# Stores of half batches 0 to 8 moved from ScalarE to SyncE, and one more step in the background work at the start of the expert layers

## The chip, the core and the metric

The kernel runs on one core of one Trainium2 chip. A core has engines that run side by side and wait for each other by semaphores: TensorE (PE, matmuls), VectorE (DVE), ScalarE (ACT), GpSimd (POOL) and SyncE (SP, which only issues transfers here). SyncE, ScalarE and GpSimd issue DMA transfers, each into a queue of its own; 16 DMA engines carry them out. The metric is the device time of one execution in microseconds (us), lower is better.

## The reference

A causal convolution of width 7 over 8 batches of 3584 tokens with 192 channels, with weights that are a softmax per head, is followed by a mixture of 8 experts. Each token is given to one expert by going through all gate logits in falling order until an expert is full (28672 / 8 = 3584 tokens).

```python
w = exp(weight - weight.max(-1)); w = w / (w.sum(-1) + 1e-9)          # 8 heads x 7
x_unf = x_pad[:, arange(S)[:, None] + arange(7)]                      # sliding windows
a = einsum('hk,bskhg->bshg', w, x_unf).reshape(N, D)                  # N = 28672, D = 192

logits = a @ w_gate                                                   # N x 8
for idx in argsort(-logits.flatten()):                                # greedy, with capacity N // 8
    tok, e = idx // E, idx % E
    if assigned[tok] < 0 and counts[e] < cap:
        assigned[tok] = e; counts[e] += 1
for e in range(E):
    m = assigned == e
    out[m] = maximum(a[m] @ w1[e], 0) @ w2[e]                         # 192 x 1024, 1024 x 192
```

All of it is float32; the kernel splits operands into high and low parts where the matmul's precision needs it.

## The kernel before

**The convolution.** The tokens are cut into 16 half batches of 1792. `load(i)` brings the half batch into one of four `X` buffers, by transfers that SyncE issues (lines 189 or 192, and 194) and, for the second half of the windows, one that ScalarE issues (line 194, put off through `later`). `conv(i)` multiplies by a Toeplitz matrix `TH`, one matmul group `cv` for each of 8 heads, ScalarE copies each result into `a` (one of three buffers), and after the last head the whole `a` is stored to `attn` in DRAM, line 214. The experts' inputs are gathered from `attn` later. Half batch 14's store is held back and issued in half batch 15. Loads run three half batches ahead: in program order stands `load(i + 3)`, then `conv(i)` with its store.

**The gate.** Beside the convolution of the next half batches, VectorE transposes `a` (`transp`, tile `aT`), TensorE makes gate logits from it (`gate(i, u)`, u = 0 to 2, tile `pl`, or `bg` when a bank of the background work is used), ScalarE brings them to tile `L`, and `end(i)` transposes `L` with one matmul (`pt<-ident,L` or `bg<-ident,L`), stores it in `LT` and reduces it (`M`).

**The routing** is background work: a list of generators, `bg = Steps(..., (half(0), tail(), half(1), rest()))`. Each `yield` in them ends a step; the main program calls for a step at places that it chooses. `half(0)` works on the tokens of the first 8 half batches while the later ones are convolved, and ends with the indices of the first tiles; its matmuls use banks named `bg` (`bg<-iq,ones` and `bg<-c_oh,X` among the last). `tail()` finishes the gate of half batches 14 and 15.

**The experts.** 56 tiles of 512 tokens, 7 for each expert: first layer `ph`, 8 groups of five matmuls; `hh` and `hl`, its high and low parts; second layer `y`. `wload` (lines 1235 to 1240) brings weights to tile `raw` by SyncE, and ScalarE and VectorE make `w` and `dl` of them. The first four pieces of these loads are called when half batch 13 begins, behind the last loads of `X` in SyncE's order. In tile 0 the main program asks for background steps three times in each of the first layer's eight groups, and only the calls whose numbers are in `TAIL = (6, 7, 8, 11, 12)` (line 1497) take one.

**What sets the order.** Each engine carries out its instructions in the order of the program. DMAs from SyncE and ScalarE take eight semaphores, DMAHW0 to DMAHW7, in turn, in the order in which the program lists them; a DMA waits until the transfer that used its semaphore before has landed. In the rows of the order below `[waits ...]` names the semaphores that an instruction waits for.

Of the kernel before, what the change touches and what calls it, by code (L numbers as in the profile page):

```python
# [18 lines left out]
PEW, PEA = "pe", "pe after act"  # L19
# [95 lines left out]
def build(ctx, tc, nc, x, weight, wg, attn, LT, wk):  # L115
# [4 lines left out]
    V, A, PE, P = nc.vector, nc.scalar, nc.tensor, nc.gpsimd  # L120
# [81 lines left out]
    def conv(i, mid, hold=None):  # L202
        t = X.pop(i)
        a = AA[i] = k.ap[i % 3].tile([128, 16, D], F32, name="a")
        o = a.rearrange("p w (h c) -> p h w c", c=24)
        for h in range(8):
            ps = k.cps.tile([128, 512], F32, name="cv")
            PE.matmul(ps[:, 0:384], TH[0:118, h], t[:, :, h * 24:(h + 1) * 24], start=True, stop=True)
            mid(h)
            A.activation(o[:, h], ps[:, 0:384].rearrange("p (w c) -> p w c", c=24), AF.Copy)  # L210
        put = partial(A.dma_start, attn[i * 1792:(i + 1) * 1792].rearrange("(g p b) d -> p g (b d)", g=4, b=4),
                      a[0:W].rearrange("p (g b) d -> p g (b d)", b=4))
        if hold is None:
            put()  # L214
        else:
            hold.append(put)
# [24 lines left out]
    def logits_t(i):  # L241
# [5 lines left out]
        A.activation(o, v, AF.Copy)  # L247

    k.load, k.conv, k.transp, k.logits, k.logits_t = load, conv, transp, logits, logits_t
    k.toeplitz, k.gate_load, k.gate_ops = toeplitz, gate_load, gate_ops  # L250
    return k
# [1248 lines left out]
def moe_kernel(ctx, tc, x, weight, wg, w1, w2, out):  # L1500
    nc = Pace(tc.nc)
# [4 lines left out]
    attn = drm.tile([NTOK, D], F32, name="attn")  # L1506
    with ExitStack() as cw:
# [52 lines left out]
        def tail():  # L1560

            end(14)
            for u in range(3):
                gate(15, u)
                yield PEA if u == 2 else None
            end(15)
            nc.sync.dma_start(r.ltab, LT)
            c1.close()
            cs.close()
            ff.wpool2(cw, 1)  # L1570
            ff.hp[1] = pool(cw, "fh1", 1, **late)
            yield

        bg = Steps(nc, r, (half(0), tail(), half(1), rest()))
        bg.keep = 3
        cs, c1, ca, cl, cc = (ExitStack() for _ in range(5))
# [20 lines left out]
        def end(i):  # L1597

            k.logits_t(i)
            r.top(i)  # L1600
# [9 lines left out]
        def gate(i, u):  # L1610
            for f in range(2 * u, 2 * u + 2):
                k.logits(i, f)
# [156 lines left out]
```

## Time and profile before

| | us |
|---|---|
| median of 3 runs | 1238.71 |
| lowest and highest run | 1238.25, 1239.27 |
| the profiled execution's own time | 1242.89 |
| its span in the profile | 1241.1 |

The profile is of one execution; times in it count from the start of the span. Engine names with a q (ACTq, SPq) are an engine's issuing of transfers. In a row of the timeline stand start and length in us, engine, line of the kernel, operation, output and inputs by the program's names, shapes, the number of instructions, and in brackets the idle time of the engine ahead of it with what ended it. Most compute instructions go through one helper and so have line 56. In the profile the conv stage lasts until about 155 us, and the tiles of the experts fill the rest.

The costliest groups of instructions (columns: line, engine, operation, tiles, count | busy us, mean ns | idle us of the engine just before them, with what ended most of it) are the experts' matmuls; the convolution's come far behind:

```profile
L56 PE MATMUL y<-w,hh 128*128 128x384 f32 x1792 | 535.7, 355 | 0.0
...
L56 PE MATMUL ph<-xa,w 128*128 128x512 f32 x1344 | 395.2, 402 | 0.4 <-DVE hl L56 0.4
...
L56 PE MATMUL cv<-X,TH 118*128 118x384 f32 x256 | 99.7, 516 | 13.9 <-DVE TH L56 12.2
```

### The profile page before, as it was taken

Reading aid. Unit: us, or ns where it says so; the run is one execution under the profiler, and the core shown is the slowest. Engines: PE = TensorE matmul, PEld = TensorE weight load, DVE = VectorE, ACT = ScalarE, POOL = GpSimd, SP = SyncE. Lnnn points to the kernel's source line nnn. Section 1 sums busy time; section 2 is a strip of 40 time slices with the busy share of each in tenths; the row PEclk is TensorE's granted clock in tenths of the full one; section 3 lists DMA queues with packets and bytes.
Section 4 is the critical chain, followed back from the end, with each engine's and each line's share of the span. In section 5 each row is a group of like instructions: output and inputs, shape, how many; then the busy total and the mean of one; then the engine's idle time right before and its main releaser. Section 6 shows DMA issues by size and latency. Waiting matters only on the chain.

```text
span 1241.1 us, 21785 instructions
## 1 busy us (share of the span) xinstructions
PE 1203.0 (97%) x7694; PEld 1033.9 (83%) x7694; DVE 984.8 (79%) x2126; ACT 559.6 (45%) x1251; POOL 532.5 (43%) x520
## 2 busy tenths in 40 slices
PE   6999899999999999999999999999999999999997
PEld 3545578889989988889888889999999999999996
DVE  7588679898998988889879856777777777777762
ACT  5544555556445454444554443343333433333332
POOL 2000234435556555555465435434544444543422
PEclk9999999999999999999999999999999999999999
DMA  9999664659427473745343442114223232423100
GB/s 249 369 347 325 202 215 121 151 159 323 140 68 215 134 244 83 255 155 184 102 130 105 126 106 70 45 39 158 94 100 105 100 101 93 155 69 125 48 24 28
DMA packets 128580, 182.00 MB, mean 147 GB/s; under 512 B 20992, under 2 KB 91088, under 8 KB 126800
## 3 DMA queue, kind: packets, MB, share of 16 engines
q1 hardware_dynamic: 85856, 104.13, 27.6%
q0 software_dynamic: 21504, 44.07, 12.0%
q10 hardware_dynamic: 21104, 32.34, 7.6%
q8 instruction: 62, 1.02, 0.3%
q14 instruction: 54, 0.44, 0.1%
HBM read 102.37 MB, written 78.12 MB: 145 GB/s over the span
## 4 chain that ended last, share of the span: by engine, by line
PE 87%; DVE 5%; DMA 4%; issue 1%; ACT 1%; ACTq 0%; SPq 0%; POOL 0%; POOLq 0%; DVEq 0%
PE ph L56 40%; PE y L56 39%; PE cv L56 4%; PE bg L56 3%; DMA attn<-a 3%; DVE X L56 1%; PE pl L56 1%; DVE TH L56 1%; DVE aT L56 1%; DVE hl L56 1%; DMA X<-otab 0%; PE px L56 0%; DMA wb<-in_weight_dram 0%; ACTq L214 0%; DMA otab<-X 0%
## 5 line engine op out<-in xcount | busy, mean ns | idle before, releaser
L56 PE MATMUL y<-w,hh 128*128 128x384 f32 x1792 | 535.7, 355 | 0.0
L56 ACT ACTIVATE hh<-ph 128x512 fp32r<-128x512 f32 x448 | 267.3, 597 | 453.1 <-PE ph L56 380.3
L56 PE MATMUL y<-w,hl 128*128 128x192 f32 x1792 | 448.9, 251 | 0.0
L56 DVE SCALAR_TENSOR_TENSOR hl<-ph,hh 128x512 fp32r<-128x512 f32 x448 | 307.6, 687 | 129.1 <-ACT hh L56 99.7
L56 PE MATMUL ph<-xa,w 128*128 128x512 f32 x1344 | 395.2, 402 | 0.4 <-DVE hl L56 0.4
L56 PEld LDWEIGHTS y<-w,hl 128*128 128x128 f32 x1792 | 340.9, 190 | 16.2
L56 PEld LDWEIGHTS y<-w,hh 128*128 128x128 f32 x1792 | 336.3, 188 | 20.9 <-issue 3.0
L1383 POOL DMA_INDIRECT out_dram<-yo,ia x128 | 144.3, 1127 | 240.2 <-DVE yo L56 195.7
L56 PEld LDWEIGHTS ph<-xa,w 128*128 128x128 f32 x1344 | 218.5, 189 | 21.6 <-issue 1.8
L1383 POOL DMA_INDIRECT out_dram<-yo,ib x96 | 94.9, 988 | 221.0 <-DVE yo L56 213.6
L56 PE MATMUL ph<-xd,w 128*128 128x512 f32 x448 | 177.3, 396 | 0.0
L1308 POOL DMA_INDIRECT xg<-attn,ja x128 | 141.5, 1106 | 78.9 <-issue 39.1
L56 PE MATMUL ph<-xd,dl 128*128 128x512 f32 x448 | 174.1, 389 | 0.2 <-issue 0.2
L56 DVE STREAM_TRANSPOSE xs<-xg 32x128 f32<-32x128 f32 (+2 forms) x408 | 164.8, 404 | 6.6
L56 ACT ACTIVATE yt<-y 128x192 f32<-128x192 f32 x224 | 73.0, 326 | 109.8 <-PE y L56 72.3
L56 DVE TENSOR_TENSOR yo<-y,yt 128x192 f32<-128x192 f32 x224 | 79.2, 354 | 49.9 <-ACT yt L56 46.6
L1308 POOL DMA_INDIRECT xg<-attn,jb x96 | 103.3, 1076 | 29.3 <-issue 29.3
L56 PE MATMUL cv<-X,TH 118*128 118x384 f32 x256 | 99.7, 516 | 13.9 <-DVE TH L56 12.2
L56 PEld LDWEIGHTS ph<-xd,dl 128*128 128x128 f32 x448 | 84.2, 188 | 20.1 <-issue 0.5
L56 PEld LDWEIGHTS ph<-xd,w 128*128 128x128 f32 x448 | 84.0, 187 | 19.6 <-issue 0.6
L56 PEld LDWEIGHTS cv<-X,TH 118*128 118x128 f32 x256 | 44.9, 195 | 43.7 <-POOL TH L152 12.0
L56 ACT ACTIVATE a<-cv 128x384 f32<-128x384 f32 x128 | 59.4, 493 | 43.1 <-PE cv L56 21.3
(237 smaller groups left out, 919.8 us busy)
## 6 DMA issues: line engine op xcount, KB each, us to landing
attn<-a ACTq DMA_DIRECT2D x16, 1344.0 KB
raw<-in_moe_w_dram SPq DMA_DIRECT2D x56, 192.0 KB
X<-in_x_dram SPq DMA_DIRECT2D x15, 672.0 KB
X<-in_x_dram ACTq DMA_DIRECT2D x15, 672.0 KB
kw<-w SPq DMA_DIRECT2D x36, 256.0 KB
kv<-w SPq DMA_DIRECT2D x24, 384.0 KB
scr<-xs SPq DMA_DIRECT2D x96, 96.0 KB
w<-kw SPq DMA_DIRECT2D x6, 1536.0 KB
```

What stands on the lines that cost most here:

```text
L56: return f(*a, **k)
L1308: self.nc.gpsimd.indirect_dma_start(out=t[:, b], out_offset=None, in_=self.attn[0:rows], in_offset=bass.IndirectOffsetOnAxis(ap=idx[b], ax ...
L1383: st = self.nc.gpsimd.indirect_dma_start(out=self.out, out_offset=bass.IndirectOffsetOnAxis(ap=idx, axis=0), in_=o, in_offset=None, bounds ...
```

## The change

The store of a half batch is issued by SyncE for half batches 0 to 8, and by ScalarE, as before, for 9 to 15. In `tail()` a `yield` is added behind `end(14)`, so that the first logits of half batch 15, `gate(15, 0)`, are a step of their own.

```diff
@@ -208,7 +208,7 @@
             PE.matmul(ps[:, 0:384], TH[0:118, h], t[:, :, h * 24:(h + 1) * 24], start=True, stop=True)
             mid(h)
             A.activation(o[:, h], ps[:, 0:384].rearrange("p (w c) -> p w c", c=24), AF.Copy)
-        put = partial(A.dma_start, attn[i * 1792:(i + 1) * 1792].rearrange("(g p b) d -> p g (b d)", g=4, b=4),
+        put = partial((nc.sync if i < 9 else A).dma_start, attn[i * 1792:(i + 1) * 1792].rearrange("(g p b) d -> p g (b d)", g=4, b=4),
                       a[0:W].rearrange("p (g b) d -> p g (b d)", b=4))
         if hold is None:
             put()
@@ -1560,6 +1560,7 @@
         def tail():
 
             end(14)
+            yield PEW
             for u in range(3):
                 gate(15, u)
                 yield PEA if u == 2 else None
```

The order of SyncE's instructions, at the end of the convolution's loads. Rows are: line, operation, output and input, shape. Before, the last loads of `X` and the first loads of the experts' weights:

```order
L192 DMA X<-in_x_dram 6x16x192 [waits DMAHW4_49,DMAHW1_49,PE_49]
L194 DMA X<-in_x_dram 112x8x192 [waits DMAHW3_49]
L1235 DMA raw<-in_moe_w_dram 128x512 [waits DMAHW4_49]
L1237 DMA raw<-in_moe_w_dram 64x512 [waits DMAHW5_49]
L1238 DMA raw<-in_moe_w_dram 64x512 [waits DMAHW6_49]
L1235 DMA raw<-in_moe_w_dram 128x512 [waits DMAHW0_49]
L1237 DMA raw<-in_moe_w_dram 64x512 [waits DMAHW1_49]
L1238 DMA raw<-in_moe_w_dram 64x512 [waits DMAHW2_49]
```

The same place in the changed kernel:

```order
L192 DMA X<-in_x_dram 6x16x192 [waits DMAHW6_49,DMAHW4_49,PE_49]
L194 DMA X<-in_x_dram 112x8x192 [waits DMAHW5_49]
L1235 DMA raw<-in_moe_w_dram 128x512 [waits DMAHW6_49]
L1237 DMA raw<-in_moe_w_dram 64x512 [waits DMAHW7_49]
L1238 DMA raw<-in_moe_w_dram 64x512 [waits DMAHW0_49]
L1235 DMA raw<-in_moe_w_dram 128x512 [waits DMAHW1_49]
L1237 DMA raw<-in_moe_w_dram 64x512 [waits DMAHW2_49]
L1238 DMA raw<-in_moe_w_dram 64x512 [waits DMAHW3_49]
```

The instructions are the same, the semaphores have shifted. Before, DMAHW6 of the first L1238 was last used by the store of half batch 10 and DMAHW2 of the second by that of half batch 11. Now DMAHW6 of the first L1235 was last used by the store of half batch 11, DMAHW1 of the second L1235 by ScalarE's last load of `X`, and DMAHW3 of the second L1238 by the store of half batch 12.

SyncE again, in the middle of the changed kernel's convolution, from the fifth store on:

```order
L214 DMA attn<-a 112x4x768 [waits DMAHW7_49,Activation_49]
L189 DMA X<-in_x_dram 6x15x192 [waits DMAHW0_49,DMAHW1_49,PE_49,Pool_49]
L194 DMA X<-in_x_dram 112x8x192 [waits DMAHW2_49]
L214 DMA attn<-a 112x4x768 [waits DMAHW3_49,Activation_49]
L192 DMA X<-in_x_dram 6x16x192 [waits DMAHW4_49,PE_49]
L194 DMA X<-in_x_dram 112x8x192 [waits DMAHW6_49]
L214 DMA attn<-a 112x4x768 [waits DMAHW7_49,Activation_49]
```

Before, this stretch had the same rows without those of L214, which stood on ScalarE.

TensorE in tile 0, from the first layer's third group on (`bg<-ident,L` is the transposition in `end`, `bg<-aT,c_mu` the logits of `gate(15, u)`). Before:

```order
L56 MATMUL px<-ident,xg 128x128 x4
L56 MATMUL bg<-ident,L 128x128
L56 MATMUL bg<-aT,c_mu 32x128 x8
L56 MATMUL ph<-xa,w_1426 128x512 x3
L56 MATMUL bg<-aT,c_mu 32x128 x8
L56 MATMUL ph<-xd,w_1426 128x512
L56 MATMUL ph<-xd,dl 128x512
L56 MATMUL bg<-aT,c_mu 32x128 x8
L56 MATMUL ph<-xa,w_1426 128x512 x3
L56 MATMUL ph<-xd,w_1426 128x512
L56 MATMUL ph<-xd,dl 128x512
L56 MATMUL bg<-ident,L 128x128
```

The same place in the changed kernel:

```order
L56 MATMUL px<-ident,xg 128x128 x4
L56 MATMUL bg<-ident,L 128x128
L56 MATMUL ph<-xa,w_1426 128x512 x3
L56 MATMUL bg<-aT,c_mu 32x128 x8
L56 MATMUL ph<-xd,w_1426 128x512
L56 MATMUL ph<-xd,dl 128x512
L56 MATMUL bg<-aT,c_mu 32x128 x8
L56 MATMUL ph<-xa,w_1426 128x512 x3
L56 MATMUL ph<-xd,w_1426 128x512
L56 MATMUL ph<-xd,dl 128x512
L56 MATMUL bg<-aT,c_mu 32x128 x8
L56 MATMUL bg<-ident,L 128x128
```

Each group of logits has moved one place back behind first layer matmuls; the second `bg<-ident,L` stands where it stood, and now directly behind the last logits. The first step of `half(1)`, which was taken at the end of the calls in tile 0, now comes when tile 1 begins.

## The prediction

> **What bounds the kernel now.** I read the page first, for the span and the busy time of each engine, then busy time by stretches of 20 us, then the chain of waits, and last the single instructions of ScalarE, SyncE and TensorE between 75 and 170 us. The page:
>
> ```profile
> span 1241.1 us, 21785 instructions
> ...
> PE 1203.0 (97%) x7694; PEld 1033.9 (83%) x7694; DVE 984.8 (79%) x2126; ACT 559.6 (45%) x1251; POOL 532.5 (43%) x520
> ...
> PE ph L56 40%; PE y L56 39%; PE cv L56 4%; PE bg L56 3%; DMA attn<-a 3%; DVE X L56 1%; PE pl L56 1%; DVE TH L56 1%; DVE aT L56 1%; DVE hl L56 1%; DMA X<-otab 0%; PE px L56 0%; DMA wb<-in_weight_dram 0%; ACTq L214 0%; DMA otab<-X 0%
> ```
>
> TensorE is busy 1203.0 of 1241.1 us. The change takes no matmul away, so what it can win or lose is idle time of TensorE, 38.1 us in all. The chain (the work that ended last, followed back) is 79% first and second layer matmuls; but 3% of it, some 30 us, goes through the stores `attn<-a`. The stretches show where TensorE is idle while the convolutions run (columns: stretch, its length, busy PE, PEld, DVE, ACT, POOL with instruction counts, granted clock, DMA share, GB/s):
>
> ```profile
> 60.00:80.00 20.00, 18.21 (x166) 9.50 (x169) 19.17 (x55) 10.41 (x27) 0.25 (x1) 1.00 1.07 344
> 80.00:100.00 20.00, 16.96 (x150) 8.71 (x138) 15.90 (x33) 8.11 (x23) 0.29 (x1) 1.00 1.07 357
> 100.00:120.00 20.00, 19.63 (x203) 12.57 (x203) 17.03 (x33) 9.52 (x25) 1.94 (x3) 1.00 1.00 305
> 120.00:140.00 20.00, 20.00 (x207) 13.32 (x210) 16.71 (x41) 12.77 (x32) 1.04 (x1) 1.00 0.91 300
> 140.00:160.00 20.00, 15.95 (x189) 10.13 (x177) 11.41 (x16) 9.03 (x25) 9.91 (x11) 1.00 0.49 153
> ```
>
> PE lacks 1.79 + 3.04 + 0.37 = 5.2 us between 60 and 120, nothing from 120 to 140, and 4.05 from 140 to 160. In 60 to 100 the DMA engines are full (share 1.07), and DVE is nearly full in 60 to 80 (19.17 of 20). ScalarE's instructions between 82 and 126 us say why PE waits (columns: start, length, instruction, and idle time before it with what ended it; ACTq is ScalarE issuing a DMA):
>
> ```profile
> 82.98 3.88 ACTq L214 DMA_DIRECT2D attn<-a  x1
> 86.96 2.02 ACT L56 ACTIVATE a<-cv 128x384 f32<-128x384 f32 x5 [4.28 <-PE bg L56]
> ...
> 92.07 3.76 ACTq L214 DMA_DIRECT2D attn<-a  x1
> 95.93 0.49 ACT L56 ACTIVATE a<-cv 128x384 f32<-128x384 f32 x1 [4.00 <-DVE aT L56]
> 96.32 0.17 ACT L56 ACTIVATE tot<-bg 128x8 bf16<-128x8 f32 x1
> ...
> 103.04 0.32 ACTq L214 DMA_DIRECT2D attn<-a  x1
> ...
> 113.66 0.32 ACTq L214 DMA_DIRECT2D attn<-a  x1
> ...
> 125.07 0.32 ACTq L214 DMA_DIRECT2D attn<-a  x1
> ```
>
> The stores of half batches 8 and 9 hold ScalarE for 3.88 and 3.76 us, those of 10, 11 and 12 for 0.32. The named releasers of the copies behind them (PE, DVE) had long been done: ScalarE was stuck in its own issue. TensorE feels it here:
>
> ```profile
> 78.23 1.56 PE L56 MATMUL cv<-X,TH 118*128 118x384 f32 x4 [0.55 <-ACT a L56]
> 87.50 1.56 PE L56 MATMUL cv<-X,TH 118*128 118x384 f32 x4 [1.04 <-ACT a L56]
> 96.55 0.40 PE L56 MATMUL bg<-U,tot 128*128 128x128 bf16 x4 [1.59 <-ACT tot L56]
> ```
>
> **The change, part one: stores 0 to 8 on SyncE.** It removes nine store issues from ScalarE. The three waits above, 0.55 + 1.04 + 1.59 = 3.2 us, follow such an issue directly; the third comes from store 9, which stays on ScalarE. I expect that it shrinks too: the issues grow long only while earlier stores are unfinished in ScalarE's queue (the chain below has store 7 landing at 92.00, just as store 9 begins its 3.76), and after the change no store is in it. DVE at 19.17 of 20 in 60 to 80 will keep some of the first wait. I take **3.0 us** that convolution 10 starts earlier; the bounds are 0 (the transfers, full at 1.07, set the pace and another wait steps in) and 5.2 (all idle time of PE from 60 to 120). On SyncE a long issue holds only the X loads behind it, and PE waits for no X transfer between 20 and 160 us; I cost that at nothing, hidden by the loads' lead. Without the lead each store would cost its issue, up to 3.88.
>
> A row bears on whether the stall leaves ScalarE at all:
>
> ```profile
> 74.48 17.52 DMA attn<-a
> ...
> 84.11 0.31 SPq L194 DMA_DIRECT2D X<-in_x_dram  x1
> ```
>
> SyncE issued an X load at 84.11 in 0.31 us, inside ScalarE's 82.98 to 86.86. So the long issue belongs to ScalarE's own queue. The Trainium skill, Perfetto Trace Analysis, section "DMA Instruction — HWDGE (DVE, Sync)", says that the descriptor generator is shared between issuing engines and locked for exclusive use while one issues. By that rule ScalarE's own X loads would stand behind SyncE's stores, and the 3.0 would be near 0; the 0.31 inside the 3.88 speaks against it.
>
> **Part one goes on: the weight loads behind the stores.** The DMAs of SyncE and ScalarE share eight semaphores in turn, and each waits for the previous user of its own. Moving nine DMAs among the others shifts who waits for whom. Before:
>
> ```profile
> 113.70 0.56 SPq L1237 DMA_DIRECT2D raw<-in_moe_w_dram x1
> 115.80 0.47 SPq L1238 DMA_DIRECT2D raw<-in_moe_w_dram x1
> 120.26 0.35 SPq L1235 DMA_DIRECT2D raw<-in_moe_w_dram x1
> 120.66 0.47 SPq L1237 DMA_DIRECT2D raw<-in_moe_w_dram x1
> 125.09 0.47 SPq L1238 DMA_DIRECT2D raw<-in_moe_w_dram x1
> ...
> SPq L1238 <- DMA attn<-a: 5.5, 2, 4.0
> ```
>
> The two L1238 loads wait for the landings of stores 10 and 11 (last line: 5.5 us in all, 2 times, 4.0 the longest). After, the first load, L1235, waits for store 11 and the last, L1238, for store 12; on SyncE the four between are queued behind the first. The last is what counts, for ScalarE converts the weights in order and the routing's small matmuls hang behind it:
>
> ```profile
> 131.48 0.63 ACT L56 ACTIVATE w<-raw 128x512 fp32r<-128x512 f32 x1 [0.47 <-DMA raw<-in_moe_w_dram]
> ...
> 133.30 0.67 DVE L56 COPY X<-bg 128x1024 bf16<-128x1024 bf16 x1
> ...
> 134.59 0.27 PE L56 MATMUL bg<-iq,ones 128*128 128x256 bf16 x1
> ```
>
> ScalarE already waits 0.47 for this load. From its start at 131.48 to DVE's end at 133.97 are 2.5 us, and TensorE, in order, comes to these matmuls at 134.59, so 0.6 later than it need. Now the new time. Store 12 was issued at 125.07; with 3.0 won, at 122.1. Its landing: the sizes are
>
> ```profile
> attn<-a ACTq DMA_DIRECT2D x16, 1344.0 KB
> ```
>
> so at the 341 to 357 GB/s of a full stretch at least 1.376 MB / 357 = 3.9 us; at most what store 11 took, which was issued at 113.66 and let L1238 go at 125.09, 11.4 us. I take 6.7: the store and the five weight loads in front (128x512 and 64x512 numbers of four bytes, 0.92 MB) are 2.29 MB at 341. That is nearer the low end because the last X loads are then nearly through. So it lands at 128.8. The load after it: at least 0.13 MB / 357 = 0.4 us, at most the 6.4 from 125.09 to 131.48; I take 2.5, near the low end, as nothing is left in front of it. ScalarE's last conversion starts at 131.3, and TensorE's matmuls can start at 131.3 + 2.5 = 133.8: 0.8 us before 134.59. **Of the 3.0 us won, 2.2 are lost in a new wait of TensorE at about 132 us, and 0.8 remain.** The bounds are -5.2 (nothing lost) and, with both far ends, 122.1 + 11.4 + 6.4 + 2.5 = 142.4, +7.8.
>
> The Trainium skill, DMA: Bandwidth & Descriptors, section "Queues, rings and completion order", says that a DMA engine takes turns between queues by packets and serves each in order. By it stores 9 to 12, alone with the X halves in ScalarE's queue, would land sooner than store 11's 11.4, and the X loads behind stores in SyncE's later; the sum would move towards the 3.0 kept. No row of before shows such a mix.
>
> **Part two: the added `yield`.** It adds no instruction. It moves the transposition's matmuls in tile 0 by a step:
>
> ```profile
> 158.51 0.41 PE L56 MATMUL bg<-aT,c_mu 128*32 128x128 f32 x4
> 159.20 0.41 PE L56 MATMUL bg<-aT,c_mu 128*32 128x128 f32 x2 [0.27 <-DVE aT L56]
> 160.06 0.62 PE L56 MATMUL bg<-aT,c_mu 128*32 128x128 f32 x10 [0.46 <-DVE aT L56]
> 160.61 0.97 PE L56 MATMUL ph<-xa,w 128*128 128x512 f32 x3
> ...
> 162.75 0.65 PE L56 MATMUL bg<-aT,c_mu 128*32 128x128 f32 x16
> ...
> 165.69 0.33 PE L56 MATMUL bg<-ident,L 128*128 128x128 f32 x1 [0.95 <-ACT L L56]
> ```
>
> TensorE waits 0.27 + 0.46 = 0.73 us for DVE's transposes. With three `ph` matmuls (0.97) ahead, this is covered: **-0.7**. The bill may come at `bg<-ident,L`: five `ph` matmuls stood between the last logits and it, now none. It waits 0.95 today although they stand there; from the end of the last logits (162.75 + 0.65) to 165.69 are 2.3 us. Bounds for this wait: 0 and 2.3 in place of 0.95; I leave it at 0.95, its own row. So part two lies between -1.7 and +0.6. The routing's later steps slip by a third of a tile; that is beside a full TensorE with nothing that waits for them soon, and I cost it at 0.
>
> **Sum.** -0.8 - 0.7 = -1.5 us on the profiled execution, which took 1242.89 us (span 1241.1 and 1.8 around it). That execution is 4.2 above the median of 1238.71; I take the difference over to the median: **1237.2 us**.
>
> **The rivals.**
> - *The weight loads do not bind.* For it: store 12 has an emptier queue before it; if it lands in 4 to 5 us, TensorE keeps all. 3.0 to 4.5 + 0.7: 1233.5 to 1235.0. Against: ScalarE waits for this load already before. Chance 0.17.
> - *The weight loads come late: slower.* Place: the last L1238 behind store 12, then `w<-raw`, then TensorE's `bg<-iq`. It decides from the point where `w<-raw` starts after 132.7 (134.59 + 0.6 - 2.5): each us later is a us of TensorE. Store 12 in 9.2 and the load in 4.4, the middle between my values and the far ends, give 135.7, so 138.2 against 134.59: +3.6 - 0.7, 1241.6. For it: DMA share 0.91 to 1.00 from 100 to 140. Chance 0.14.
> - *The stores' move wins nothing in the convolutions*, because DMA at 1.07 sets the pace, or the generator is locked as in the rule above. Then store 12 is at 125.07, the conversion at 134.3, TensorE at 136.8: +2.2 - 0.7, 1240.2. Against: 84.11. Chance 0.12.
> - The forecast, -3.5 to +1.0 about 1237.2: 0.57.
>
> **How the numbers follow.** Faster by over 0.2% (2.5 us, about what a measurement here can tell from no change): the first rival and the fast edge of the forecast, 0.17 + 0.17 = 0.34. Slower: the second rival and a corner of the third, 0.16. The rest, 0.50, is within. The range for 8 in 10 runs from 1233.8, inside the first rival, to 1241.2, short of the far half of the second; the ends with both far prices (+7.8) I leave out as less than 3 in 100.
>
> **What would show it.** ScalarE has no L214 issue before store 9, and store 9 takes some 0.3. The waits at 87.50 and 96.55 are gone and PE's busy time in 80 to 100 rises from 16.96 to 19 or more. A new wait of 1 to 3 us appears before `bg<-iq` or in the convolution beside it, released through `w<-raw`, with L1238 issued late at about 129. In tile 0 the waits of 0.27 and 0.46 are gone. I am wrong if 120 to 140 stays full of TensorE work, or if TensorE waits for X.

## The result, and the profile after

The changed kernel takes **1248.25 us** (median of 6 runs, 1247.77 to 1249.42) against 1238.99 for the kernel before in 6 runs beside it (1238.25 to 1240.8): a ratio of **1.0074**, 95% interval 1.0061 to 1.0087. It is 0.74% slower. The forecast was 1237.2 us and its range ended at 1241.2. The profiled execution after took 1248.38 us, 0.1 above its median. That of before lay 3.9 above its median, so the two spans differ by 5.4 us and not by 9.3.

From the page of the changed kernel, the lines that answer to those of before; the last is the group of the convolution's matmuls (busy us, mean ns, idle us before them):

```profile
span 1246.5 us, 21787 instructions
...
PE 1204.9 (97%) x7694; PEld 1035.1 (83%) x7694; DVE 986.3 (79%) x2126; ACT 562.1 (45%) x1251; POOL 533.9 (43%) x520
...
L56 PE MATMUL cv<-X,TH 118*128 118x384 f32 x256 | 102.9, 528 | 25.8 <-DVE TH L56 12.7
```

The same 256 matmuls have 25.8 us of idle time before them (13.9 before), and take 102.9 us in place of 99.7. On the page's chain `DMA X<-in_x_dram` stands with 3%, where before, of the transfers, only the stores had such a share. By stretches of 20 us (columns as before):

```profile
60.00:80.00 20.00, 19.31 (x161) 9.61 (x159) 19.17 (x54) 10.10 (x27) 0.25 (x1) 1.00 1.07 355
80.00:100.00 20.00, 18.97 (x172) 9.95 (x171) 18.06 (x40) 9.46 (x27) 0.36 (x1) 1.00 1.02 328
100.00:120.00 20.00, 14.02 (x145) 8.91 (x144) 13.97 (x22) 6.24 (x17) 1.94 (x3) 1.00 1.06 307
120.00:140.00 20.00, 15.53 (x141) 10.65 (x140) 10.85 (x22) 7.69 (x18) 0.00 (x0) 0.98 0.92 271
140.00:160.00 20.00, 16.35 (x161) 9.30 (x162) 12.32 (x30) 9.53 (x24) 7.96 (x8) 0.85 0.48 146
```

From 60 to 100 TensorE gains what the prediction expected: its idle time falls from 4.83 to 0.69 + 1.03 = 1.72 us. From 100 to 140, where it lacked 0.37, it now lacks 5.98 + 4.47 = 10.45. The first expert tile begins at 167.35 us, 11.9 later than before (155.47). What follows it, up to the end, takes 1079.2 us against 1085.6. From 180 to 800 us TensorE is idle for 6.8 us in the profile of before and 3.2 in that of after, so a part of this difference is that the execution profiled before lay above its median; the loss itself lies ahead of tile 0. TensorE's waits, and the start of tile 0:

```profile
94.48 0.40 PE L56 MATMUL bg<-U,tot 128*128 128x128 bf16 x4 [0.26 <-ACT tot L56]
102.31 1.53 PE L56 MATMUL cv<-X,TH 118*128 118x384 f32 x4 [2.06 <-DMA X<-in_x_dram]
108.07 1.56 PE L56 MATMUL cv<-X,TH 118*128 118x384 f32 x4 [1.59 <-ACT a L56]
116.07 1.53 PE L56 MATMUL cv<-X,TH 118*128 118x384 f32 x4 [2.33 <-DMA X<-in_x_dram]
138.28 0.98 PE L56 MATMUL cv<-X,TH 118*128 118x384 f32 x2 [4.47 <-ACT a L56]
...
167.35 0.96 PE L56 MATMUL ph<-xa,w 128*128 128x512 f32 x3
...
171.95 0.62 PE L56 MATMUL bg<-aT,c_mu 128*32 128x128 f32 x10 [0.43 <-DVE aT L56]
...
176.91 0.33 PE L56 MATMUL bg<-ident,L 128*128 128x128 f32 x1 [1.16 <-ACT L L56]
```

Two of the long waits are for loads of `X`, and one is for a free buffer of `a`. The chain of waits through that place (start, length, what) tells how the loads came late, and two rows of SyncE and ScalarE show where the 4.47 comes from:

```profile
91.22 12.97 DMA attn<-a
...
104.20 11.73 DMA X<-in_x_dram
...
127.14 12.78 DMA attn<-a
...
139.94 2.75 DMA raw<-in_moe_w_dram
```

```profile
125.84 0.35 SPq L1235 DMA_DIRECT2D raw<-in_moe_w_dram  x1
...
136.74 0.63 ACT L56 ACTIVATE w<-raw 128x512 fp32r<-128x512 f32 x1 [6.85 <-DMA raw<-in_moe_w_dram]
```

Store 9, issued by ScalarE at 91.22, lands 12.97 us later. Only then does SyncE issue the `X` load at 104.20, although it needs nothing of that store: the two use the same semaphore. Its 0.69 MB take 11.73 us, and TensorE waits 2.33 at 116.07. The first weight load, L1235, waits in the same way for store 11 (4.0 us) and is issued at 125.84, 13 us later than before (112.80). It lands only at 136.7: ScalarE has stood still for it for 6.85 us, the copy of a convolution stands behind it in ScalarE's order, and TensorE waits 4.47 for that copy. The last weight load, on the chain above, waits for store 12; TensorE's waits behind it are 0.74 us at 143.83 and 0.38 at 145.12. But the lag is older than these waits. The transfers from 20 to 60 us in slices of 1 us, before and then after:

```profile
GB/s 257 242 256 260 290 303 409 396 398 382 402 396 406 353 343 369 328 325 358 345 376 386 392 397 389 380 359 247 351 396 376 373 390 387 396 391 386 392 355 296
DMA packets 12584, 14.23 MB, mean 356 GB/s; under 512 B 284, under 2 KB 10523, under 8 KB 12580
```

```profile
GB/s 256 236 252 257 263 213 193 291 220 339 407 412 337 329 290 156 254 314 388 399 418 386 375 340 245 309 387 390 376 359 362 302 231 242 360 366 392 389 392 382
DMA packets 11549, 12.81 MB, mean 320 GB/s; under 512 B 252, under 2 KB 9771, under 8 KB 11545
```

**By 60 us the changed kernel has moved 1.42 MB less**, about one store of 1.38 MB, while TensorE has lost only 0.5 us in this stretch (39.19 of 40 busy, 39.68 before). Both kernels begin near 250 GB/s, with loads alone; before reaches 400 in the seventh slice, after in the eleventh, and it falls back to 156 at 35. The chain and SyncE's queue say why:

```profile
30.70 11.97 DMA X<-in_x_dram
...
42.69 0.02 SPq L214
...
42.73 10.05 DMA attn<-a
```

```profile
24.62 0.31 SPq L214 DMA_DIRECT2D attn<-a  x1
...
42.73 0.31 SPq L214 DMA_DIRECT2D attn<-a  x1
...
52.85 5.24 SPq L214 DMA_DIRECT2D attn<-a  x1
```

Store 2, issued at 34.15 before, now stands in SyncE's queue behind `X` loads, the last of which is issued at 37.48 in 0.49 us, and then waits 4.7 us more for the semaphore of a load that ScalarE had issued at 30.70. It starts at 42.73, 8.6 us later; store 0 is 3.4 later (24.62 against 21.23).

The packets tell loads and stores apart, since those of 512 B to 2 KB are the loads' (768 B) and those of 2 to 8 KB the stores' (3072 B). Counted so, these megabytes were moved from 20 us to the time at the head of the column, in before, after and the kernel of experiment 10 below:

| | 40 us | 60 us | 100 us |
|---|---|---|---|
| loads: before, after, exp. 10 | 3.92, 3.80, 3.07 | 7.86, 7.31, 6.66 | 15.15, 13.92, 13.14 |
| stores: before, after, exp. 10 | 2.86, 1.98, 3.66 | 6.32, 5.45, 5.83 | 12.97, 12.42, 12.70 |

In the changed kernel the stores are late first, by 0.88 MB at 40 us. When they come through, the loads fall behind, by 0.55 MB at 60 us and 1.23 at 100. SyncE's half of the load for half batch 11 is issued at 89.64 (76.71 before) and that for 12 at 104.20 (84.11 before).

### The profile page after: what moved, and what is told of

It reads as the page before. It is cut to its first block, busy times and chain, and to the rows that moved or that the text cites. A ratio compares the mean times of both kernels' runs of the same rounds, so it can differ in the third digit from the quotient of the medians.

```text
span 1246.5 us, 21787 instructions
## 1 busy us (share of the span) xinstructions
PE 1204.9 (97%) x7694; PEld 1035.1 (83%) x7694; DVE 986.3 (79%) x2126; ACT 562.1 (45%) x1251; POOL 533.9 (43%) x520
## 3 DMA queue, kind: packets, MB, share of 16 engines
q0 software_dynamic: 21504, 44.07, 11.9%
## 4 chain that ended last, share of the span: by engine, by line
PE 88%; DMA 6%; DVE 3%; ACT 1%; issue 1%; POOL 0%; POOLq 0%; SPq 0%; ACTq 0%; DVEq 0%
PE ph L56 41%; PE y L56 39%; PE cv L56 3%; DMA X<-in_x_dram 3%; DMA attn<-a 3%; PE bg L56 3%; DVE TH L56 1%; PE pl L56 1%; DVE X L56 1%; PE px L56 0%; DVE hl L56 0%; DMA wb<-in_weight_dram 0%; DVE aT L56 0%; ACT hh L56 0%; DMA raw<-in_moe_w_dram 0%
## 5 line engine op out<-in xcount | busy, mean ns | idle before, releaser
L56 PEld LDWEIGHTS ph<-xa,w 128*128 128x128 f32 x1344 | 218.6, 189 | 20.1 <-issue 1.0
L56 PE MATMUL cv<-X,TH 118*128 118x384 f32 x256 | 102.9, 528 | 25.8 <-DVE TH L56 12.7
```

The costliest lines, as they stand in the source:

```text
L56: return f(*a, **k)
```

## The experiments

Each kernel was timed beside the kernel before on its chip, and the ratio is to that; the chips differ by about 1%. Edits are shown against the kernel before, unless another is named.

**1 and 2. One part alone.** The first has only the `yield`, the second only the stores on SyncE.

```diff
             end(14)
+            yield PEW
```

```diff
-        put = partial(A.dma_start, attn[...
+        put = partial((nc.sync if i < 9 else A).dma_start, attn[...
```

> Only the added yield; all stores stay on ScalarE. My step on part two: -0.7 us against before (the waits of 0.27 and 0.46 in tile 0 shrink, nothing else moves), so within 0.2% of before. Both theories on the loss of the changed kernel, the semaphores one (SyncE's loads are held by shared semaphores that a recent store used) and the queue one (any store in SyncE's order holds up the X loads behind it), say the same here: between -1.5 and +0.5. Rival: the yield itself brings part of the loss, +2 us or more.

> Only the stores 0 to 8 on SyncE, without the yield. Both theories: the whole loss, 1247 to 1250 where before is at 1239, with SyncE's load of half batch 12 late behind the landing of store 9, the last L1238 behind store 12, and TensorE 4 us idle near 135. If the yield brought part of the loss: 1246 or less.

The `yield` alone: 1228.81 against 1230.24, ratio 0.9989 (0.9978 to 1.0001). The stores alone: 1239.42, ratio 1.0070 (1.0046 to 1.0094). The whole loss is the stores'. TensorE's long waits with the stores alone stand at the same places as those of the changed kernel:

```profile
101.18 1.85 PE L56 MATMUL cv<-X,TH 118*128 118x384 f32 x4 [1.97 <-DMA X<-in_x_dram]
114.14 1.53 PE L56 MATMUL cv<-X,TH 118*128 118x384 f32 x4 [1.51 <-DMA X<-in_x_dram]
137.50 1.65 PE L56 MATMUL cv<-X,TH 118*128 118x384 f32 x2 [5.62 <-ACT a L56]
```

The `yield` alone was measured once more:

> The added yield alone once more, for its sign: 0.9989 with an interval of 0.9978 to 1.0001 was measured. My term of -0.7 us says 0.9994; if the yield is worth nothing, 1.000.

1228.47 against 1229.55, ratio 0.9989 (0.9980 to 0.9999): the `yield` is worth about 0.1%, with an interval that ends just below 1, and it is the only version here that is not slower than before.

**3 and 4. Other semaphores.** GpSimd's transfers take none of the eight semaphores, so stores 0 to 8 there take ScalarE's stall away without SyncE. With eight stores on SyncE in place of nine, the semaphores fall otherwise.

```diff
+        put = partial((P if i < 9 else A).dma_start, attn[...
```

```diff
+        put = partial((nc.sync if i < 8 else A).dma_start, attn[...
```

> Stores 0 to 8 issued by GpSimd, without the yield: they leave ScalarE, and do not enter SyncE's order; GpSimd's DMAs use other semaphores, so X loads and weight loads share the eight among themselves and with stores 9 on. Semaphores and queue theory alike: the 3 us won between 60 and 100 stay, and nothing of the loss comes: 1235.5 to 1237.5 where before is at 1239. Rival: the transfers themselves (DMA share 1.07) are the limit whoever issues them, or GpSimd's queue is slow: 1239 or more, with TensorE waiting for X or for the buffer of a between 95 and 120.

> Stores 0 to 7 on SyncE (8 on ScalarE), without the yield. Eight of nine stores still stand in SyncE's order, but the semaphores fall otherwise: no X load of SyncE waits for store 9, and the last L1238 waits for an X load and not for store 12 (the first L1237 waits for store 11, L1237 of the second pair for the last X load of ScalarE). Semaphores theory: most of the loss gone, at most 1242 where before is at 1239. Queue theory: most of the loss stays, 1245 to 1249, with SyncE's issues of stores as long as in the changed kernel and TensorE waiting for X after 100.

On GpSimd: 1236.19, ratio 1.0056 (1.0029 to 1.0083), with the wait for `X` already in the first third:

```profile
36.09 2.90 PE L56 MATMUL cv<-X,TH 118*128 118x384 f32 x4 [3.14 <-DMA X<-in_x_dram]
```

None of these stores stands in SyncE's order, so that order is not the only thing that can make the loads late. Eight on SyncE: 1236.67, ratio 1.0050 (1.0033 to 1.0067). The waits through the weight loads shrink to four of about 1 us or less, but a wait for `X` of 3.78 us stands at 94.36. The semaphore of one particular load is a part of the loss at most.

**5. The weight loads out of the way.** The changed kernel, with the first six weight loads on GpSimd, where no store holds them.

```diff
+        dq = nc.gpsimd if self.loaded < 4 else nc.sync
...
-            nc.sync.dma_start(t, self.w1[e, 0:128, s])
+            dq.dma_start(t, self.w1[e, 0:128, s])
... (the two loads of kind "d" in the same way)
```

> The changed kernel, with the first six weight loads (the first four pieces of wload) issued by GpSimd, whose DMAs use other semaphores. Semaphores theory on the second half of the loss: ScalarE's wait for the last raw (6.85 and more in the changed kernel) and TensorE's 4.5 us near 135 go, and the slow clock after them (0.70 to 0.88 at 136 to 144): 5 to 8 us less than the changed kernel, a ratio to before of 1.001 to 1.004; the waits for X at 102 and 116 stay. Rival: the weight loads are late because the transfers themselves are (share 1.05 or more), whoever issues them: 1.006 or more.

1248.80 against 1243.14, ratio 1.0052 (1.0035 to 1.0069). The wait of 4.47 is gone, and in its place stands one for `X`, 20 us earlier:

```profile
117.34 2.90 PE L56 MATMUL cv<-X,TH 118*128 118x384 f32 x4 [5.56 <-DMA X<-in_x_dram]
```

**6 and 7. Another order of the same transfers.** The changed kernel with both big loads of `X` on ScalarE from half batch 4 on; and the changed kernel with each of stores 0 to 8 listed behind the next load on SyncE. Against the changed kernel:

```diff
-            part(nc.sync, 0, 8)
-            later.append(partial(part, A, 8, 8))
+            if i < 4:
+                part(nc.sync, 0, 8)
+                later.append(partial(part, A, 8, 8))
+            else:
+                later.append(lambda: (part(A, 0, 8), part(A, 8, 8)))
```

```diff
+        if i < 9:
+            k.pend.append(put)
...
                 k.load(i + 3, later)
+            while k.pend:
+                k.pend.pop(0)()
```

> The changed kernel, with both big halves of the X loads from half batch 4 on issued by ScalarE, so that SyncE holds the stores and the small first rows of X alone, and no big X load stands behind a store. Order theory (X loads stand behind stores in SyncE's order and queue): TensorE's waits for X at 41, 57, 74, 82, 102 and 116 go, and what is behind them comes earlier: ratio to before 0.997 to 1.003. Rival, transfers: DMA is full from 20 to 120 and any order that gives the stores more turns takes them from X; the waits for X stay, or turn into waits for the buffer of a: 1.005 or more.

> The changed kernel, with each store 0 to 8 listed behind the next X load on SyncE instead of ahead of it. Order theory: the load no longer waits for a store's issue of 5 us and its bytes stand ahead of the store's; the waits for X at 102 and 116 go (in this order no X load waits for store 9 by a shared semaphore before half batch 13): ratio to before at most 1.003. Rival, transfers: the waits for X shrink but the stores land later and ScalarE waits longer for the buffer of a: 1.005 or more.

The first: 1257.99, ratio 1.0123 (1.0103 to 1.0143); now ScalarE is stuck in its issues of loads, and TensorE waits for the logits that it copies, up to 5.35 us. The second: 1250.60, ratio 1.0061 (1.0044 to 1.0078). No wait for `X` is left, but convolutions wait for a buffer of `a` that the later store frees, 3.34 us here and 2.74 at 111.90:

```profile
40.57 1.56 PE L56 MATMUL cv<-X,TH 118*128 118x384 f32 x4 [3.34 <-ACT a L56]
```

**8 and 9. A pair on GpSimd.** Stores 0 to 8 and ScalarE's loads of `X` for half batches 4 to 12 on GpSimd, so that the pair which shared a queue before shares one again, without ScalarE; then the same with the `yield`.

```diff
-            later.append(partial(part, A, 8, 8))
+            later.append(partial(part, P if 4 <= i <= 12 else A, 8, 8))
+        put = partial((P if i < 9 else A).dma_start, attn[...
```

> The kernel before, with stores 0 to 8 and the second halves of X of half batches 4 to 12 both issued by GpSimd: two queues with the same transfers as before, but the queue with the stores is not ScalarE's. Mix theory: loads keep a store beside them as before, so 20 to 100 us moves at 350 GB/s or more, and ScalarE's issues no longer hold its copies: ratio to before 0.996 to 0.999. Rival (any queue other than ScalarE's for the stores costs X its turns, as GpSimd's did): 1.003 or more.

> The same with the added yield. 0.1% less than the run without it (e1_yield measured 0.9989 for the yield alone): 0.995 to 0.998. Rival: 1.002 or more.

1265.05 against 1243.08, ratio 1.0163 (1.0136 to 1.0191), and 1258.90, 1.0126 (1.0110 to 1.0143). One of SyncE's own small loads now took 10.99 us to issue (at 35.57), and TensorE waited 7.27 for `X` at 49.51.

**10. Is ScalarE's stall a cost at all?** The kernel before with the `yield`, and with every `X` load from half batch 4 on issued by SyncE, so that the stores are alone in ScalarE's queue.

```diff
-            later.append(partial(part, A, 8, 8))
+            later.append(partial(part, nc.sync if i >= 4 else A, 8, 8))
```

> The kernel before with the yield, and with all X loads from half batch 4 on issued by SyncE; ScalarE issues the stores alone. Each queue then carries about one half of the bytes, loads keep their lead (nothing but loads stands in SyncE's order), and a store has only stores in front of it in ScalarE's queue. Full-DMA theory: loads and stores run side by side, 20 to 100 us moves 28 MB or more, ScalarE's long issues of 2 to 4 us shrink: ratio to before 0.995 to 0.999. Rival (loads in one queue get half of the turns and lose their lead, as in f2_swap): 1.003 or more.

1241.17 against 1229.55, ratio 1.0090 (1.0075 to 1.0105). A store issue and TensorE's long waits:

```profile
79.51 0.33 ACTq L214 DMA_DIRECT2D attn<-a  x1
```

```profile
44.55 2.58 PE L56 MATMUL cv<-X,TH 118*128 118x384 f32 x4 [3.66 <-DMA X<-in_x_dram]
...
141.10 1.65 PE L56 MATMUL cv<-X,TH 118*128 118x384 f32 x2 [7.01 <-ACT a L56]
```

The stall is wholly gone, without any store on SyncE, and the kernel is slower than before by more than the changed one. So the stall was not time that could simply be had back. The table above shows what happened instead: at 40 us the stores are 0.80 MB ahead of before's and the loads 0.85 behind. As this version also puts all loads into one queue, it does not tell the two apart.

**11 and 12. Room for the transfers.** Before and after, each with three of a half batch's eight `cv` groups issued twice (48 matmuls more, the output unchanged), so that TensorE needs longer for a half batch than the transfers do.

```diff
+            if h in (1, 4, 7):
+                PE.eng.matmul(ps[:, 0:384], TH[0:118, h], t[:, :, h * 24:(h + 1) * 24], start=True, stop=True)
```

> The kernel before, with three of the eight convolution matmuls of each half batch issued twice (48 of them; the output is unchanged): 2.3 us more of TensorE for each half batch, so that it needs some 10 us and the transfers of a half batch (8 to 9 us) fit in. About 37 us more than before, 1.028 to 1.031, and the DMA engines below full from 60 us on. It is the other half of the next run.

> The changed kernel with the same doubled matmuls. SyncE's order and most of the shared semaphores are those of the changed kernel. Full-DMA theory (the move of the stores costs because the DMA engines are full and the new arrangement moves less): with room in them the loss is gone: between 4 us less and 1 us more than h1_before_slow (the stalls of ScalarE's issues, if any are left there, are saved, and the yield gives its 0.1%). Rival (the order of SyncE's instructions and the semaphores hold loads up by themselves, whatever the load of the DMA engines): 5 us or more above h1_before_slow, as the changed kernel is 9 above before.

1251.71 and 1252.26 us (before 1230.49): **the difference of 9.3 us has become 0.55.** The added matmuls cost 21.2 us and not the 37 expected: up to tile 0 TensorE is busy for 27 us more than in the profile of before, and idle for 11.8 in place of 21.1. The stretch from 20 to 60 us of the two, before's version first:

```profile
20.00:60.00 40.00, 40.00 (x263) 21.92 (x262) 18.25 (x28) 19.05 (x45) 2.98 (x10) 1.00 1.07 323
```

```profile
20.00:60.00 40.00, 40.00 (x264) 21.93 (x263) 17.75 (x28) 19.37 (x46) 3.02 (x10) 1.00 1.00 286
```

TensorE is full in both, and yet the second moves 37 GB/s less, 1.5 MB in 40 us. So the lag comes from where the stores are issued, not from TensorE's waits. At 100 us 1.3 MB of it is still there (23.62 MB against 24.90 since 20 us), but TensorE never runs into it: it is full from 100 to 140 us in both. Where there is room, the lag costs next to nothing. As one version has the `yield` and the other not, up to 2 us of the stores' cost may remain.

**13 to 15. The rates of the transfers alone.** Small kernels with loads of half an `X` (pieces of 768 B) and stores of `a` (3072 B), in stretches one after the other; the rest of the computation is left out, and the output is ones.

> Transfers alone, without the computation (the output holds ones): X halves and stores of the kernel's shapes in five stretches: (A) loads on SyncE's queue alone, (B) loads with the halves on two queues, (C) stores alone, (D) loads with the store in ScalarE's queue, as before, (E) loads with the store in SyncE's queue, as in the changed kernel. Mix theory (loads without a store beside them move less at the same full DMA engines): A and B 215 to 270 GB/s, C about 400, and D and E 330 to 360, with a lower rate the longer loads run alone. Rival (the rate depends on the size of packets alone, and a queue's share on who issues): B much faster than A, or D and E at the mean of A and C by time, about 300.

> Transfers alone again, this time with each engine's DMAs in the order written (in g1_rates ScalarE's stores went out beside the first loads, so that the stretches overlapped): (A) loads on SyncE's queue, (B) halves on two queues, (C) stores alone, (D) loads, with the stores and the second halves in ScalarE's queue as before, (E) loads, with stores and first halves in SyncE's queue. Mix theory: A 215 to 250, B 240 to 270, C 390 to 410, D 330 to 360 GB/s, E in between, 290 to 360. Rival: A and B at 350 or more, so that loads alone are no slower than loads beside a store.

> Transfers with engines at work (the output holds ones): six half batches of loads with the halves on two queues, four times: with nothing else, with TensorE at fp32 matmuls, with VectorE at transposes, with both; then stores alone, and loads and stores, both with both engines at work. h3_rates measured loads alone at 288 to 298 GB/s; in the changed kernel stretches of loads without stores run at about 240. Theory (the engines' traffic in the on-chip memory slows the loads): 290 in the first stretch, 230 to 260 in one of the next three. Rival (something else in the kernel): 285 to 298 in all four.

In the first the stretches ran into each other, and it was replaced by the second. There, loads on one queue and then on two (25 to 75 us), stores alone, and two mixes, with loads and stores on the queues that they have before (to 145) and after:

```profile
25.00:75.00 50.00, 1.64 (x11) 0.00 (x0) 1.00 1.10 292
75.00:90.00 15.00, 0.91 (x6) 0.00 (x0) 1.00 1.03 403
96.00:145.00 49.00, 0.44 (x3) 0.00 (x0) 1.00 1.06 335
145.00:188.00 43.00, 1.41 (x11) 0.00 (x0) 1.00 0.99 322
```

Loads move at 292 GB/s and stores at 403; the mixes, at 335 and 322, are no faster than the same bytes of each kind one after the other, 2 / (1/292 + 1/403) = 338. That mixing as such makes transfers faster was a theory, and it falls. The third kernel let TensorE, VectorE or both work beside the loads: 286 to 303 GB/s in every slice of 5 us at a DMA share of 1.10, so such work does not bring the loads down to the 250 of the kernel.

The megabytes that each version moved from 20 to 60 us, beside its ratio:

| version | MB | ratio |
|---|---|---|
| before | 14.23 | 1 |
| `yield` alone, two runs | 14.14, 14.16 | 0.9989 |
| after | 12.81 | 1.0074 |
| stores on SyncE, no `yield` | 13.01 | 1.0070 |
| eight stores on SyncE | 12.96 | 1.0050 |
| stores on GpSimd | 12.95 | 1.0056 |
| after, weight loads on GpSimd | 12.94 | 1.0052 |
| after, store behind the next load | 12.63 | 1.0061 |
| after, big loads on ScalarE | 12.60 | 1.0123 |
| all loads on SyncE | 12.54 | 1.0090 |
| pair on GpSimd | 12.59 | 1.0163 |
| pair on GpSimd, with the `yield` | 12.58 | 1.0126 |

The four versions with stores on SyncE and little else changed have TensorE busy for 39.2 to 39.5 of these 40 us (after, no `yield`, eight stores, weight loads on GpSimd), so there the lag comes ahead of the waits. In the six other slower versions TensorE already waits here (32.1 to 36.9 busy), and their bytes are in part a consequence. Experiments 3 and 6 to 10 had been expected to win the time back, and each came out on the side of its rival; 5 came out between the two.

## Why the prediction was wrong, step by step

**ScalarE's relief: right in kind, smaller in size.** No store issue is left on ScalarE before store 9, and that one takes 0.32 us. TensorE's idle time from 60 to 100 shrinks by 3.1 us. But the changed kernel came into this stretch behind, with 0.5 us less of TensorE's work done in the first 20 us and 0.5 in the next 40; so `bg<-U,tot` and store 10 both start 2.07 us earlier (94.48 and 100.97), where 3.0 were expected for convolution 10.

**"I cost that at nothing, hidden by the loads' lead": the step that failed.** The prediction had the long issues on SyncE (they came: 5.24 us at 52.85) and the loads behind them, and trusted the trace of before, which has no wait for `X` from 20 to 160 us. It never asked how large the lead was, nor how a store waits when it stands in order behind loads. TensorE waiting for `X` was on its list of signs of being wrong, but had no price and no chance. Stores 0 and 2 lose 3.4 and 8.6 us in SyncE's queue, the transfers fall 1.42 MB behind by 60 us, and at about 350 GB/s (before from 60 to 100 us) that is 4.1 us. First the stores are late, then the loads; SyncE's half of load 12 is issued 20.1 us later than before. TensorE waits for `X` 5.8 us between 20 and 175: four times for 0.3 to 0.4 while it lives on the lead, and then, from 100 us on, 2.06 and 2.33. Experiment 2 ties the loss to the stores, 12 shows the lag without any wait of TensorE, and shows it harmless where there is room. The DMA share of 1.07 had been read as a bound on the gain (the third rival), but not as a resource that a new order can use worse.

**The stall as pure waste: wrong.** Experiment 10 removes it in another way and loses 0.9%. There the stores go through sooner than before and the loads later (3.66 and 3.07 MB at 40 us, 2.86 and 3.92 before). In the changed kernel it is the other way round at first: the stores come late, and the loads pay when they catch up. That ScalarE's long issues in before keep a good balance between the two is suggested by this, not shown; what balance would be best was not tried. That an issue grows long only behind unfinished stores was too narrow as well: in experiment 10 SyncE's queue holds loads alone, and one of the small loads takes 5.70 us to issue (at 29.29).

**The weight loads: right group, wrong load.** The prediction let the last L1238 decide, and put the wait of TensorE at 2.2 us. That load does wait for store 12 and then takes 2.75 us (2.5 expected). Store 12 was issued at 127.14 and not at 122.1, and landed in 12.78 us and not in 6.7, beyond the far end of 11.4. But TensorE's 4.47 was over at 138.28, before the last L1238 was even issued at 139.94. It came from the first load, L1235: the prediction saw that it would wait for store 11, but gave it no price. It was issued at 125.84, took 10.9 us to land, beside store 12, and ScalarE, in order, stood still for it. The thought that stores 9 to 12, with fewer others in ScalarE's queue, might land sooner than 11.4 us did not come true for store 9 (12.97) nor for store 12. This is the place of the second rival (slower), yet not the whole cause: with the weight loads moved away (experiment 5), the loss is still 0.52%, and the wait stands at an `X` load. What the weight loads add is then about the step from 0.52 to 0.74%, and the two intervals overlap.

**The `yield`: right in sign.** -0.7 was expected, from -1.7 to +0.6; -1.1 and -1.4 were measured. Only the wait of 0.27 is gone, 0.43 stays of 0.46, and `bg<-ident,L` waits 1.16 after and 0.55 in the kernel with the `yield` alone, against 0.95. In that kernel the three changes make 0.70; what more was measured lies within the noise.

**The rule on the locked generator.** SyncE's issue and ScalarE's, after:

```profile
54.52 0.32 ACTq L194 DMA_DIRECT2D X<-in_x_dram  x1
```

ScalarE issued a load in 0.32 us inside SyncE's 52.85 to 58.09. As with 84.11 before, the long issue belongs to the queue, not to a shared part. The Trainium skill's rule of exclusive use (Perfetto Trace Analysis, "DMA Instruction — HWDGE (DVE, Sync)") is not what these rows show.

**A part of the loss that no step had: the clock.** Behind some waits of TensorE the granted clock (the column after POOL) is lower:

```profile
136.00:140.00 4.00, 1.72 (x11) 1.39 (x12) 2.46 (x4) 2.52 (x5) 0.00 (x0) 0.88 0.51 185
140.00:144.00 4.00, 3.26 (x15) 2.04 (x13) 2.85 (x4) 2.24 (x5) 0.00 (x0) 0.70 0.54 154
...
156.00:160.00 4.00, 4.00 (x19) 1.84 (x22) 3.53 (x5) 1.76 (x5) 3.12 (x4) 0.57 0.28 77
```

Before had 1.00 in all of these. The busy time times what is missing from the clock gives 0.2 + 1.0 + 1.7 = 2.9 us, which fits the 3.2 by which the convolution's busy time grew. The 1.7 follow a wait of 2.53 us at 155.79 which before has too, 2.63 at 144.60 with the clock left at 1.00; no run shows that the change brings this part. The sum up to tile 0: TensorE's idle time grew from 21.1 to 29.4 us and its busy time from 134.4 to 138.0, together the 11.9. Experiments 1 and 2, on one chip, repeat it: tile 0 begins at 150.65 with the `yield` alone and at 161.62 with the stores alone, which have 5.9 us more of idle and 5.1 more of busy time up to there.

**What stays open.** Why loads without a store beside them move at about 250 GB/s in this kernel (20 to 24 us, both versions) and at 292 alone was not found: neither the number of queues nor the work of the engines explains it. Nor was it settled how much of the lag is the order in SyncE's queue and how much the shared semaphores. For store 2 both count: 3.8 of its 8.6 us pass until the loads ahead are issued, and 4.7 in its own wait for an earlier load. With the stores on GpSimd, neither in SyncE's order nor on the eight semaphores, the loss is of a similar size.

## What to carry to other kernels

Before a transfer moves to another queue, ask what stands ahead of it there, in order and by semaphore, and how many bytes the stretch can fall behind before someone waits: the absence of a wait in the trace does not say how large the lead is. Where the transfers set the pace, an engine that is stuck in its issues may be holding back the transfers that are less urgent; look at the bytes moved by a given time, of each kind, for they showed this loss 40 us before the first long wait. And to tell whether such a loss is a lack of slack, make the computation beside the transfers longer: here the lag stayed and the loss went away.

## What the runs showed of the hardware

A DMA share of about 1 does not tell how much is moved: it stood at 1.07 with 323 GB/s and with 356, and at 1.10 with 292.

Some waits of TensorE were paid twice, by the wait and by a lower clock behind it: the 4.47 us went with 0.88 and 0.70 in the two stretches to 144. The length alone did not decide it. The stores alone had 0.78 from 100 to 104, around a wait of 1.97 us, and the changed kernel 0.57 behind 2.53, while it kept 1.00 around 2.06 (at 102.31), and the kernel before kept 1.00 around 2.63. The Trainium skill, "TensorE: Matmul & The Clock Gate", section "Part 1: The HAM clock gate (the "warmup" mystery)", gives half clock after at least one idle window of about 3.4 us. The 4.47 agrees with that; the 1.97 and the 2.53 are shorter than the window.
